# Splitting the first load, turning the taps earlier and re-ordering an SSM convolution and SwiGLU kernel on Trainium2

## The chip, the cores and the metric

The kernel runs on one core of one Trainium2 chip. The time is device time in microseconds (us), the median of three runs. A core has four compute engines that work side by side: TensorE (PE in the profile; its weight loads are listed as PEld), VectorE (DVE), ScalarE (ACT) and GpSimd (POOL). SyncE (SP) issues most transfers; a transfer issued by ACT stands in ACT's queue. The order of the instructions on each engine is written out by the program; the engines meet through semaphores.

## The reference

Sequences of 2048 rows with 512 channels go through two rounds of a convolution block A and a gated feed-forward block B, with the same weights in both rounds:

```python
def _A_ref(q, k, v, shift_k, ssm_k, ssm_D):
    k_shift = sum of k_pad[:, t:t + S, :] * shift_k[:, 3 - t] over the 4 taps
    kv = k_shift * v
    y = irfft(rfft(kv padded to 2S) * rfft(ssm_k padded to 2S))[:S] + kv * ssm_D
    return q * y

def _B_ref(x, w_gate, w_up, w_down):
    return (silu(x @ w_gate) * (x @ w_up)) @ w_down

x = A_q
x = x + _A_ref(layernorm(x), A_k, A_v, A_shift_k, A_ssm_k, A_ssm_D)
x = x + _B_ref(layernorm(x), B_w_gate, B_w_up, B_w_down)
x = x + _A_ref(layernorm(x), A_k, A_v, A_shift_k, A_ssm_k, A_ssm_D)
x = x + _B_ref(layernorm(x), B_w_gate, B_w_up, B_w_down)
```

(The first line of A and the FFT lines are condensed.) The tensors are bf16; w_gate and w_up are 512 x 1792, w_down is 1792 x 512. The convolution's result y is the same in both rounds, so it is computed once.

## The kernel before

**Tiling.** The 2048 rows are four blocks of 512 (NB = 4). In a block, partition p holds the rows 4p to 4p+3 (R = 4), so a block is a tile of 128 partitions x 4 rows x 512 channels. A unit of the feed-forward is (layer, block, half), two of the four rows of a block: 16 units of 256 rows.

**Convolution.** The long convolution is done in blocks. Each block of the filter h (ssm_k) and of kv gets a small Fourier spectrum by matmuls with cosine and sine tables (`fwd`, whose transposes `inv` serve the way back). Products of spectra are formed and added up on DVE, and matmuls with `inv` give y. h comes with channels on the partitions, and PE transposes it to `hs` (L511; copies out of PSUM at L521 to L527). The skip term D is added to row 0 of h there (`drow`, L524). k is transposed in the same way (L400, copies L406/L408) to `kT`, which has a pad of zeros in front (L394).

**The four taps.** `shift_mul` (L531) computes the shifted sum of k on PE: per row and per group of 128 channels (dt = 0 to 3), four matmuls of kT with a diagonal matrix `dg` that carries one tap of 128 channels. The taps are loaded as rows (`tapR`, L1087), turned on PE (L1153), copied to `tapT` and `tapF` on DVE (L1155, L1156), and 16 diagonals are made from the identity (L1166 to L1173), dt by dt on the engine that the string DGE names: D for DVE, A for ACT, P for POOL. The product with v (L558) gives kv.

**Feed-forward.** The normalised x is transposed to zT. For each pair of 128 columns of the 1792, PE computes gate and up (L997, recorded at the helper line L345), ACT applies SiLU (L1000) and copies up to ht (L1004), DVE multiplies (L1007), and PE adds up the down projection in PSUM (L1020). Elsewhere ACT copies the result to dn (L1056) and DVE adds it to x (L1059). In the last unit, (1, 3, 1), the residual x is put into PSUM first by matmuls with the identity (L979); the second of its two rows is split into two halves of 256 channels, one in `pds[1]`, one in `pds[2]`, and its last copies (L1027, L1033) write x straight from PSUM, with the output transfers at L1029 and L1036.

**Order.** The code first lists all operations (`plan.add`), each with its engine, an estimated cost, an estimated latency for transfers (`lat`), and what it reads and writes. ORDER gives each operation its position in one sequence; `Plan.order` sorts by it and places the operations in time by the estimates, `Plan.issue` (L251) writes them out in that sequence. So ORDER fixes each engine's queue, and the buffers of each ring follow from it. LH0 and LK0 are the estimated latencies of the first h and the first k.

**Fillers.** In `issue`, where PE's planned start lies more than 0.5 us behind its last end and before 32 us, matmuls on constants (`wm`, L1288) are written in, one per 0.106 us of planned gap. They go to the first PSUM slot, in the order pf, pd, pc, that is free at that time.

**The start of the queues.** ACT issues the loads of the taps and of drow. SP issues h of block 0 (L376, 512 KB in one transfer, since H_SPLIT is False), k, v, x of block 0, h and v of block 1, the gate weights, the two transposes of the tables (L1177), then k of block 1 and the other weights. POOL makes constants and the identity, then three diagonals, the pad of kT and a fourth diagonal.

Of the kernel before, what the change touches and what calls it, by code (L numbers as in the profile page):

```python
# [29 lines left out]
LH0 = 3.6  # L30
LK0 = 4.3
# [8 lines left out]
DGE = 'DDAP'  # L40
SHE = "DDDD"
PAIRS = ((0,), (2,), (1,), (3,))
H_SPLIT = False
# [8 lines left out]
    4, 74, 3, 1, 2, 22, 16, 12, 14, 0, 13, 15, 40, 7, 6, 5, 8, 9, 17, 11, 18, 19, 10, 20, 21, 25, 41, 42, 56, 57, 34, 35, 33, 36, 31, 32, 29, 30, 51,  # L52
    53, 52, 70, 38, 39, 45, 48, 23, 24, 26, 64, 60, 46, 44, 61, 55, 43, 66, 76, 73, 47, 37, 82, 27, 28, 62, 63, 58, 68, 54, 65, 49, 50, 59, 69, 79,
    168, 199, 216, 243, 275, 75, 93, 94, 95, 96, 80, 89, 90, 91, 92, 77, 78, 81, 84, 85, 97, 98, 99, 100, 101, 104, 103, 105, 110, 125, 134, 147, 148,
    149, 166, 178, 71, 102, 111, 116, 117, 119, 120, 121, 67, 87, 83, 88, 72, 86, 106, 107, 108, 109, 112, 113, 114, 130, 131, 132, 144, 145, 146,
    139, 140, 141, 135, 136, 137, 126, 127, 128, 118, 122, 124, 123, 115, 133, 152, 155, 161, 156, 170, 175, 138, 129, 153, 154, 142, 143, 150, 151,
    158, 160, 157, 163, 159, 164, 171, 179, 162, 165, 197, 198, 188, 211, 212, 213, 176, 167, 177, 182, 219, 227, 169, 173, 172, 174, 180, 181, 183,
    184, 189, 190, 228, 229, 208, 209, 191, 231, 210, 185, 195, 186, 192, 193, 187, 196, 194, 202, 203, 220, 224, 225, 226, 221, 222, 238, 223, 230,
    232, 242, 233, 246, 247, 268, 263, 269, 267, 270, 271, 273, 274, 272, 281, 283, 284, 304, 316, 317, 311, 312, 248, 255, 257, 256, 259, 258, 261,
    260, 214, 215, 234, 205, 206, 207, 200, 201, 204, 217, 218, 236, 325, 326, 235, 249, 321, 324, 295, 296, 308, 309, 290, 292, 299, 300, 237, 285,  # L60
    327, 329, 354, 355, 368, 367, 276, 302, 375, 613, 303, 262, 305, 319, 320, 353, 369, 373, 374, 418, 432, 413, 433, 434, 460, 459, 465, 502, 473,
    495, 494, 514, 522, 524, 556, 557, 523, 542, 536, 500, 581, 650, 626, 651, 264, 265, 244, 245, 239, 240, 250, 251, 266, 323, 322, 252, 253, 241,
    254, 278, 288, 286, 287, 289, 336, 331, 291, 294, 293, 306, 297, 298, 279, 280, 307, 337, 332, 301, 310, 313, 314, 315, 338, 333, 339, 334, 342,
    352, 366, 350, 351, 360, 361, 346, 357, 378, 422, 399, 386, 387, 402, 403, 385, 388, 364, 365, 407, 423, 430, 406, 411, 404, 405, 384, 395, 396,
    397, 412, 424, 431, 340, 341, 344, 345, 371, 437, 439, 438, 440, 441, 347, 343, 348, 356, 349, 358, 359, 370, 376, 377, 381, 382, 383, 389, 391,
    390, 393, 394, 409, 410, 419, 420, 414, 415, 451, 452, 444, 445, 453, 461, 463, 462, 464, 466, 467, 471, 470, 472, 476, 477, 501, 545, 496, 544,
    447, 450, 448, 449, 488, 489, 487, 492, 493, 509, 506, 468, 469, 491, 498, 479, 481, 456, 457, 499, 510, 534, 482, 511, 454, 486, 504, 512, 474,
    475, 517, 537, 535, 518, 519, 505, 515, 541, 584, 563, 585, 596, 624, 667, 625, 427, 421, 428, 458, 478, 484, 485, 528, 530, 532, 533, 551, 553,
    538, 540, 554, 564, 573, 574, 565, 567, 400, 503, 277, 282, 531, 560, 599, 561, 619, 620, 622, 623, 621, 648, 649, 661, 662, 723, 689, 724, 318,
    330, 335, 328, 362, 380, 392, 379, 363, 398, 372, 401, 436, 480, 483, 490, 416, 417, 408, 426, 442, 443, 425, 429, 521, 548, 598, 597, 552, 601,  # L70
    603, 618, 529, 507, 513, 516, 497, 446, 435, 520, 569, 526, 571, 508, 455, 525, 527, 539, 555, 572, 578, 617, 612, 580, 579, 652, 641, 727, 728,
    717, 718, 683, 688, 676, 677, 665, 684, 643, 644, 642, 656, 731, 732, 733, 734, 778, 765, 769, 781, 674, 543, 750, 1069, 668, 657, 670, 671, 697,
    678, 698, 699, 796, 790, 805, 806, 807, 834, 835, 846, 880, 847, 891, 895, 888, 881, 892, 894, 889, 890, 896, 910, 902, 905, 925, 900, 926, 938,
    943, 949, 996, 995, 999, 1000, 1023, 1006, 1024, 1067, 582, 583, 591, 592, 568, 586, 558, 559, 600, 610, 629, 590, 595, 549, 550, 588, 589, 593,
# [31 lines left out]
    1498, 1495, 1496, 1500, 1501, 1470, 1493, 1502, 1508, 1507, 1503, 1504, 1479, 1480, 1494, 1499, 1491, 1492, 1509, 1510, 1511, 1481, 1482, 1460,  # L106
    1461, 1483, 1522, 1520, 1532, 1538, 1539, 1561, 1540, 1551, 1555, 1535, 1536, 1513, 1519, 1533, 1534, 1514, 1523, 1537, 1552, 1556, 1521, 1530,
    1515, 1516, 1528, 1529, 1524, 1525, 1531, 1553, 1557, 1543, 1544, 1526, 1527, 1541, 1542, 1548, 1549, 1550, 1554, 1562, 1545, 1546, 1517, 1518,
    1547, 1558, 1563, 1566, 1559, 1560, 1564, 1565, 1567, 1568,
]  # L110
R = 4

# [1209 lines left out]
```

## Time and profile before

| | us |
|---|---|
| median of 3 runs (344.92 to 345.08) | 344.96 |
| the profiled execution: its own time | 345.11 |
| its span (first to last record) | 343.3 |
| PE busy | 338.7 |
| DVE busy | 282.3 |
| ACT busy | 253.2 |
| POOL busy | 39.7 |
| first transposes of h on PE | 4.83 |
| first FFN matmul on PE | 33.45 |
| last matmul issued, end of PE's work | 340.3 |

The profile describes one execution. A timeline row gives the start and the length in us, the engine, the line of the code, the operation, "output<-inputs", shapes and how many were merged; in brackets, how long the engine sat idle before it and what released it. "SPq" and "ACTq" are DMA issues. A row of the chain of waits has only start, length, engine, tile and line. The end of a matmul is modelled, so a row of n matmuls lasts longer than n times their rate by the depth of the pipe; the starts are measured.

### The profile page before, as it was taken

The page shows a single profiled execution, that of the slowest core. Times are in us where ns is not written, and L with a number is a line of the kernel's source. Part 1 is how long each engine was busy: PE and PEld are TensorE (multiplying, and loading weights), DVE is VectorE, ACT ScalarE, POOL GpSimd, SP SyncE. Part 2 cuts the span into 40 slices and gives each one's busy share as a digit, 9 for nine tenths or more (in the row PEclk, how much of TensorE's full clock was granted, in tenths as well). Part 3 has the DMA queues.
Part 4 walks back from the last instruction along what each step waited for, and adds up shares of the span by engine and source line. Part 5 has one row for each costly group of instructions (what it writes and reads, how often), then busy time and mean ns, then how long its engine had stood idle before and what let it go on. Part 6 is the DMA issues. An engine that isn't in the chain of part 4 may idle for free.

```text
span 343.3 us, 6617 instructions
## 1 busy us (share of the span) xinstructions
PE 338.7 (99%) x2624; PEld 248.5 (72%) x2624; DVE 282.3 (82%) x481; ACT 253.2 (74%) x505; POOL 39.7 (12%) x46
## 2 busy tenths in 40 slices
PE   8999999999999999999999999999999999999996
PEld 7747867768686767768587768768675877777684
DVE  7999999999999999999999999989987523637030
ACT  6899999999984868867999955959464654546271
POOL 4000110103010101221010100100601000000000
PEclk9999999999999999999999999999999999999999
DMA  7999016130117156010101057000101010100001
GB/s 289 326 317 320 3 28 98 31 94 0 34 31 124 36 119 124 7 26 2 32 18 32 15 153 93 15 18 0 33 0 43 18 52 2 31 15 17 15 17 47
DMA packets 42089, 22.96 MB, mean 67 GB/s; under 512 B 33861, under 2 KB 39882, under 8 KB 42058
## 3 DMA queue, kind: packets, MB, share of 16 engines
q1 hardware_dynamic: 41904, 22.47, 26.3%
q8 instruction: 20, 0.33, 0.4%
q14 instruction: 11, 0.09, 0.1%
q10 hardware_dynamic: 154, 0.07, 0.1%
HBM read 12.33 MB, written 2.10 MB: 42 GB/s over the span
## 4 chain that ended last, share of the span: by engine, by line
PE 66%; DVE 29%; ACT 2%; issue 1%; DMA 1%; DVEq 0%
PE pf L345 38%; PE pd L1020 18%; PE ps L345 6%; DVE ht L1007 4%; DVE bnst L843 3%; DVE t L687 3%; DVE t L691 3%; DVE t L699 2%; DVE m L574 2%; DVE Z L701 2%; PE ps L492 2%; DMA zT<-z 1%; PE ps L831 1%; PE wm L1288 1%; DVE ka L642 1%
## 5 line engine op out<-in xcount | busy, mean ns | idle before, releaser
L345 PE MATMUL pf<-zT,wg_sb 128*128 128x256 bf16 x896 | 110.1, 273 | 0.1
L345 PE MATMUL pf<-zT,wu_sb 128*128 128x256 bf16 x896 | 109.6, 273 | 0.1
L1020 PE MATMUL pd<-wd_sb,ht 128*128 128x512 bf16 (+1 forms) x462 | 104.2, 373 | 0.0
L345 PEld LDWEIGHTS <-wg_sb 128*128 128x128 bf16 x896 | 87.6, 98 | 16.6 <-issue 0.6
L345 PEld LDWEIGHTS <-wu_sb 128*128 128x128 bf16 x896 | 87.6, 98 | 16.2 <-DMA zT<-z 0.5
L1004 ACT CAST ht<-pf 128x512 bf16<-128x512 f32 x112 | 64.5, 591 | 22.1 <-PE pf L345 21.8
L1000 ACT ACTIVATE sg<-pf 128x512 bf16<-128x512 f32 x112 | 65.8, 605 | 17.2 <-PE pf L345 13.4
L1020 PEld LDWEIGHTS <-ht 128*128 128x128 bf16 x462 | 45.1, 98 | 44.2 <-DVE ht L1007 0.6
L1007 DVE TENSOR_TENSOR ht<-ht,sg 128x1024 bf16<-128x1024 bf16 (+1 forms) x64 | 39.1, 618 | 22.5 <-ACT sg L1000 18.7
L848 POOL TENSOR_TENSOR rstd<-ve,nhalf 128x2 f32<-128x2 f32 x24 | 27.7, 1155 | 211.0 <-DVE ve L846 201.5
L1056 ACT CAST dn<-pd 128x512 bf16<-128x512 f32 x30 | 17.3, 591 | 31.9 <-PE pd L1020 21.8
L843 DVE BATCH_NORM_STATS2 bnst<-xc 128x6 f32<-128x512 bf16 x48 | 31.6, 685 | 0.7
L687 DVE TENSOR_TENSOR t<-X,G 128x2048 bf16<-128x2048 bf16 x18 | 22.0, 1220 | 0.1
L691 DVE TENSOR_TENSOR t<-X,G 128x2048 bf16<-128x2048 bf16 x18 | 21.9, 1217 | 0.0
L1059 DVE TENSOR_TENSOR xc<-xc,dn 128x1024 bf16<-128x1024 bf16 x15 | 10.2, 681 | 11.6 <-ACT dn L1056 11.6
L453 ACT ACTIVATE X<-ps 128x512 bf16<-128x512 f32 x32 | 19.2, 608 | 0.7 <-PE ps L492 0.5
L874 POOL TENSOR_TENSOR rstd<-ve,nhalf 128x2 f32<-128x2 f32 x8 | 8.6, 1075 | 60.5 <-ACT ve L872 60.5
L920 DVE TENSOR_TENSOR n<-n,Yk 128x1024 bf16<-128x1024 bf16 x15 | 10.3, 690 | 6.4 <-ACT Yk L725 5.4
L701 DVE TENSOR_TENSOR Z<-Z,t 128x2048 bf16<-128x2048 bf16 x12 | 14.7, 1224 | 0.3
L699 DVE TENSOR_TENSOR t<-t,t 128x2048 bf16<-128x2048 bf16 x12 | 14.7, 1223 | 0.3
L453 ACT ACTIVATE H<-ps 128x512 bf16<-128x512 f32 x24 | 13.9, 618 | 0.0
L345 PE MATMUL ps<-hs,fwd 128*128 128x512 bf16 x40 | 12.8, 379 | 0.5 <-ACT hs L521 0.3
(105 smaller groups left out, 323.7 us busy)
## 6 DMA issues: line engine op xcount, KB each, us to landing
hn<-in_A_ssm_k_dram SPq DMA_DIRECT2D x4, 512.0 KB, 5.3
vt<-in_A_v_dram SPq DMA_DIRECT2D x4, 512.0 KB, 5.2
xc<-in_A_q_dram SPq DMA_DIRECT2D x4, 512.0 KB, 6.0
out_dram<-xc SPq DMA_DIRECT2D x15, 128.0 KB, 1.8
wg_sb<-in_B_w_gate_dram SPq DMA_DIRECT2D x1, 1792.0 KB
wu_sb<-in_B_w_up_dram SPq DMA_DIRECT2D x1, 1792.0 KB, 7.6
wd_sb<-in_B_w_down_dram SPq DMA_DIRECT2D x1, 1280.0 KB, 12.7
kn<-in_A_k_dram SPq DMA_DIRECT2D x1, 512.0 KB, 4.4
```

Source lines behind the costliest of these rows:

```text
L345: nc.tensor.matmul(o, lhsT=lhsT, rhs=rhs, start=(n == 0), stop=(n == len(terms) - 1))
L453: add("ACT", act(D), lambda: nc.scalar.activation(out=view(), in_=ps.t[:], func=ACT.Copy, scale=scale), r=[ps], w=[(buf, keys)], conv=conv)
L687: dve(n * D, lambda t1=t1, part=part: nc.vector.tensor_mul(out=t1.t[:], in0=x.t[:, sl, 0, :], in1=g.t[:, sl, part, :]), [(x, key(slots, (0 ...
L691: dve(n * D, lambda t2=t2, part=part: nc.vector.tensor_mul(out=t2.t[:], in0=x.t[:, sl, 1, :], in1=g.t[:, sl, 1 - part, :]), [(x, key(slots ...
L699: dve(n * D, lambda t1=t1, t2=t2, comb=comb: nc.vector.tensor_tensor(out=t1.t[:], in0=t1.t[:], in1=t2.t[:], op=comb), [t2], [t1], conv=conv)
L701: dve(n * D, lambda t1=t1, part=part: nc.vector.tensor_add(out=z.t[:, sl, part, :], in0=z.t[:, sl, part, :], in1=t1.t[:]), [t1], [zk], con ...
L843: add("DVE", 0.6, lambda st=st, i=i: nc.vector.bn_stats(out=st.t[:], in_=xs[c].t[:, i, :]), r=[(xs[c], (i,))], w=[st])
L848: add("POOL", pw, lambda: nc.gpsimd.tensor_tensor(out=rstd.t[:], in0=ve.t[:], in1=nhalf.t[:].to_broadcast((P, n)), op=ALU.pow), r=[ve, nha ...
L1000: add("ACT", act(D), lambda ps=ps, o=o, sg=sg: nc.scalar.activation(out=sg.t[:, o:o + 2, :], in_=ps.t[:], func=ACT.Silu), r=[ps], w=[(sg, ...
L1004: add("ACT", act(D), lambda ps=ps, o=o, ht=ht: nc.scalar.copy(out=ht.t[:, o:o + 2, :], in_=ps.t[:]), r=[ps], w=[(ht, (o // 2,))], due=(uni ...
L1007: dve(n * W, lambda sg=sg, ht=ht: nc.vector.tensor_mul(out=ht.t[:], in0=ht.t[:], in1=sg.t[:]), [sg], [ht], due=(unit, k / pairs, 0.0, "h"))
L1020: nc.tensor.matmul((pds[o] if not cs.start else pds[HP]).t[:, cs], lhsT=ht.t[:, q, o * P:(o + 1) * P], rhs=wt["d"].t[:, ft, cs], start=(ft ...
```

## The change

- **First h in two transfers** (H_SPLIT = True): channels 0 to 255, then 256 to 511, 256 KB each, issued one behind the other by SP. PE transposes each row of h in two operations, one per half. The estimated latencies of h and k change with it.
- **Taps turned at once:** the estimated latency of their load goes from 2.6 to 1.1, so that the plan sees them earlier.
- **Diagonals:** DGE goes from 'DDAP' to 'DPAP'; the four of dt = 1 move from DVE to POOL, which makes eight.
- **Fillers** go to the free PSUM slot whose next use lies furthest ahead.
- **Last unit:** only the second half of the second row gets its residual by an identity matmul. The first row and the first half of the second are added by DVE when their sums are done; ACT copies the last half.
- **ORDER** is a new table for all operations (1573 instead of 1569).

```diff
-LH0 = 3.6
-LK0 = 4.3
+LH0 = 3.35
+LK0 = 4.0
...
-DGE = 'DDAP'
+DGE = 'DPAP'
...
-H_SPLIT = False
+H_SPLIT = True
...
 ORDER = [
-    4, 74, 3, 1, 2, 22, 16, 12, 14, 0, 13, 15, 40, 7, 6, 5, 8, 9, 17, 11, 18, 19, 10, 20, 21, 25, 41, 42, 56, 57, 34, 35, 33, 36, 31, 32, 29, 30, 51,
+    1, 127, 7, 0, 3, 9, 17, 2, 8, 4, 5, 6, 50, 51, 11, 13, 10, 12, 14, 18, 19, 16, 15, 22, 27, 28, 38, 43, 52, 53, 59, 30, 44, 55, 33, 46, 47, 29, 40,
...
     def issue(self, seq, place, when, warm_until, warm):
         t, busy = 0.0, {}
+        slots = [(r, i) for r in ("pf", "pd", "pc") for i in range(self.rings[r])]
...
             if o.eng == "PE":
-                if start < warm_until and start - t > 0.5:
-                    for ring, i in [(r, i) for r in ("pf", "pd", "pc") for i in range(self.rings[r])]:
-                        if busy.get((ring, i), 0.0) <= t:
-                            n = int((start - max(t, 0.3)) / 0.106)
-                            if n > 0:
-                                warm(ring, i, n)
-                            break
+                n = int((start - max(t, 0.3)) / 0.106)
+                free = [s for s in slots if busy.get(s, 0.0) <= t]
+                if start < warm_until and start - t > 0.5 and n > 0 and free:
+                    nxt = {s: 1e9 for s in free}
+                    for b, i in place.items():
+                        a = min(when[q][0] for q in b.ops)
+                        if (b.ring, i) in nxt and a >= t:
+                            nxt[b.ring, i] = min(nxt[b.ring, i], a)
+                    warm(*max(free, key=nxt.get), n)
...
         if b == 0 and H_SPLIT:
+            o = None
             for n in range(2):
                 sl = slice(2 * n, 2 * n + 2)
                 o = add(eng, 0.5, lambda sl=sl: q.dma_start(out=hn[b].t[:, sl], in_=h3[:, sl, 0:L]), w=[(hn[b], (n,))],
-                        lat=LH0 - 0.75 if n == 0 else LH0 - 0.45, due=due, after=after)
+                        lat=LH0 - 1.0 if n == 0 else LH0 - 0.45, due=due, after=list(after) + [o] * n)
...
-        if xpe:
+        if unit == LAST_UNIT:
+            cs, i = slice(D // 2, D), row(h, HP - 1)
+            add("PE", pe(1, D // 2), lambda: nc.tensor.matmul(pds[HP].t[:, cs], lhsT=ident.t[:], rhs=x.t[:, i, cs], start=True, stop=False),
+                r=[(x, (i,)), ident], w=[pds[HP]], due=(unit, 2 / pairs, 1.9, None))
+        elif xpe:
...
-                                                 start=(ft == 0 and not xpe), stop=(ft == NF - 1))
+                                                 start=(ft == 0 and not (cs.start if unit == LAST_UNIT else xpe)), stop=(ft == NF - 1))
...
-            add("ACT", act(D), lambda: nc.scalar.copy(out=x.t[:, row(h, 0), :], in_=pds[0].t[:]), r=[pds[0]], w=[(x, (row(h, 0),))],
-                due=(unit, 1.0, 3.0, "h"))
+            add("DVE", tt1(D), lambda: nc.vector.tensor_add(out=x.t[:, row(h, 0), :], in0=x.t[:, row(h, 0), :], in1=pds[0].t[:]), r=[pds[0]],
+                w=[(x, (row(h, 0),))], due=(unit, 1.0, 3.0, "h"))
...
-                copy = nc.scalar.copy if eng == "ACT" else nc.vector.tensor_copy
-                add(eng, 0.35, lambda cs=cs, copy=copy, half_=half_: copy(out=x.t[:, i, cs], in_=pds[HP if half_ else o].t[:, cs]), r=[pds[HP if half_ else o]],
+                def finish(cs=cs, half_=half_):
+                    if half_:
+                        nc.scalar.copy(out=x.t[:, i, cs], in_=pds[HP].t[:, cs])
+                    else:
+                        nc.vector.tensor_add(out=x.t[:, i, cs], in0=x.t[:, i, cs], in1=pds[o].t[:, cs])
+                add(eng, 0.35, finish, r=[pds[HP if half_ else o], (x, (i,))],
...
         tr = add("ACT", 0.42, lambda: nc.scalar.dma_start(out=tapR.t[:], in_=A_shift_k.rearrange("(dt p) j -> dt p j", p=P)), w=[tapR],
-                 lat=2.6, due=-71)
+                 lat=1.1, due=-71)
```

## The prediction

> **What bounds the kernel now.** I read the page's busy times first, then the chain of waits of the first 36 us, the stage table, the timeline of the start and the timeline of the last 12 us.
>
> ```profile
> PE 338.7 (99%) x2624; PEld 248.5 (72%) x2624; DVE 282.3 (82%) x481; ACT 253.2 (74%) x505; POOL 39.7 (12%) x46
> ```
>
> PE is busy for 99% of the span, but its ends are modelled, so I check it by rate. In the chain, eight 256-column matmuls take 0.87 us and four of 512 columns 0.86 us, so 0.109 and 0.2157 us each.
>
> ```profile
> 43.64 0.87 PE pf L345 x8
> 63.21 0.86 PE pd L1020 x4
> 221.75 5.13 PE L1020 MATMUL pd<-wd_sb,ht 128*128 128x512 bf16 x23
> 226.93 1.05 PE L345 MATMUL pf<-zT,wu_sb 128*128 128x256 bf16 x8
> 243.27 1.89 PE L1020 MATMUL pd<-wd_sb,ht 128*128 128x512 bf16 x8
> 245.27 1.47 PE L345 MATMUL pf<-zT,wg_sb 128*128 128x256 bf16 x12
> ```
>
> The last four lines are timeline rows. 221.75 + 23 x 0.2157 = 226.71, and PE goes on at 226.93: 0.22 us lost to the DMA of zT. 243.27 + 8 x 0.2157 = 245.00, next 245.27: 0.27 us lost. From the first FFN matmul (33.45) to the end (340.3) I find no other loss over 0.1 us. So after 33.45 an edit counts only if it takes PE work away, or makes or fills a wait of PE; the DVE work saved there is free.
>
> ```profile
> 13.86:26.59 12.73, 12.34 (x75) 6.11 (x74) 12.54 (x25) 11.74 (x24) 0.72 (x1) 1.00 1.11 292
> 26.59:33.45 6.86, 6.85 (x86) 5.13 (x85) 6.43 (x17) 6.86 (x16) 0.81 (x1) 1.00 1.03 348
> ```
>
> ```profile
> 13.86 0.69 DVE L558 TENSOR_TENSOR vt<-ps,vt 128x512 bf16<-128x512 f32 x1 [0.20 <-PE ps L345]
> ```
>
> Two stages (their length, then busy PE, PEld, DVE, ACT, POOL) and a timeline row. From the last product kv (L558, 13.86) to the first FFN matmul DVE is busy 12.54 of 12.73 and 6.43 of 6.86 us, with only work that leads to the first z (spectra, products, sums, statistics). So the FFN starts 19.6 us after that DVE product, whatever PE does meanwhile; and the product waits for PE's shift matmuls, which stand behind the transposes of h. PE itself loses about 1.5 us to waits and 0.55 us to ten fillers between 22.4 and 31.5.
>
> ```profile
> 0.76 2.83 PE L1288 MATMUL wm<-const-bfloat16-1.0 128*128 128x128 bf16 x25 [0.76 <-PEq L1306]
> 3.52 0.29 PE L1153 MATMUL pt<-ident,tapR 4*128 4x4 bf16 x4
> 3.74 1.03 PE L1288 MATMUL wm<-const-bfloat16-1.0 128*128 128x128 bf16 x8
> 4.83 1.18 PE L511 MATMUL pt<-ident,hn 128*128 128x128 bf16 x16
> 5.38 1.07 ACT L521 COPY hs<-pt 128x512 bf16<-128x512 bf16 x2 [0.87 <-PE pt L511]
> ```
>
> h was issued at 0.72 and landed 3.6 us later, at 4.3; PE turned it from 4.83. The fillers (wm) go at about 0.106 us each, half the speed of the transposes of k later (12 in 0.83 us).
>
> **The end: -0.32 us.** Three identity matmuls (L979: one of 512 columns, two of 256) become one of 256. 0.2157 + 0.109 = 0.32 us of PE's stream goes. Does it show at the end?
>
> ```profile
> 333.60 0.38 PE L979 MATMUL pd<-xc,ident 128*128 128x512 bf16 x1
> 333.81 2.75 PE L1020 MATMUL pd<-wd_sb,ht 128*128 128x512 bf16 x12
> 334.42 0.69 DVE L1007 TENSOR_TENSOR ht<-ht,sg 128x1024 bf16<-128x1024 bf16 x1 [0.44 <-ACT ht L1004]
> 340.09 0.42 DVE L1033 CAST xc<-pd 128x256 bf16<-128x256 f32 x1 [4.99 <-PE pd L1020]
> 340.31 0.37 ACT L1033 CAST xc<-pd 128x256 bf16<-128x256 f32 x1 [0.72 <-PE pd L1020]
> ```
>
> The last h tile is ready at 335.11. PE has ten other matmuls for that row in front of it (333.81 + 10 x 0.2157 = 335.97), 0.86 us of cover, more than the 0.32 taken. Behind the last matmul the ACT copy of the second half (0.37) and its transfer stay. The first half becomes a DVE add out of PSUM: the trace has none of 256 columns, but at 512 columns an operation with a PSUM and an SBUF operand (L558, 0.69) costs what a one-operand copy does (L408, 0.69), so I take the 0.42 of the present cast; twice that would end at 340.09 - 0.32 + 0.84 = 340.6, about where ACT's half ends. The row-0 add (0.69 for ACT's 0.59) starts near 338.7 and is done before DVE is wanted at 339.8. With the cover gone this part would be worth nothing: 0 to -0.32.
>
> **The start: -0.1 us (-0.6 to +0.4).**
> - h in two transfers. The bytes are the same; SP issues one DMA more (0.46 + 0.06 us), so k, v, x, the second blocks and wg are issued 0.5 us later. k landed 4.4 us after its issue at 1.24, 1.3 us after h, as long as its 512 KB need behind h; v and x follow likewise. Their data, not their issue, set these landings: 0. Behind wg SP issues the two transposes of the tables (4.53 to 15.99), which then begin some 0.25 us later. The second lands 13.1 us after its issue at 10.3, at 23.4; the first inverse matmul is at 24.11. Cover 0.7, then 0.45; without it, 0.25 us on PE.
> - Fillers. Their number follows the gaps of the written plan, at one per 0.106 us (a count that the code fixes, no time of the chip). The planned arrival of the taps moves from 0.42 + 2.6 to 0.42 + 1.1, so 14 of the 25 before the turn go; some 10 stand between it and the first half of h (planned 0.5 + 2.35 = 2.85), and 6 before the second half (planned 1.1 + 2.9 = 4.0). The taps' packets had all moved by 2.0 us, so the turn comes near 2.1 instead of 3.52. Then: 10 fillers to 3.4; eight transposes of the first half at the slow 0.107, to 4.3; 6 fillers to 4.9; the second half, r3 and r1 first, from 4.9 instead of 4.83. The first copy to hs (5.38 now) comes at about 5.4, though the last transposes end some 0.5 us earlier. What the early half gains, slow transposes and fillers eat. Without them r3 would be ready 0.3 and r2 0.75 us sooner: -0.6 is my bound for a start that follows the landings.
> - The new filler slot (the free one whose next use is furthest off). Now h's first transpose waits for the fillers to drain out of its own slot: last filler at 3.74 + 7 x 0.103 = 4.46, transpose at 4.83, 0.26 us more than one filler. That wait goes: -0.2, within the -0.6.
> - Diagonals. tapF comes after three of the second four phase operations, near 3.1 + 0.17; POOL starts at about 3.45 instead of 4.45. By the new order it makes six diagonals, the pad of kT, two more: 3.45 + 8 x 0.61 + 0.15 = 8.5. The first shift matmul, which reads the pad (7.3), is at 9.65 now, and those of the third and fourth POOL diagonals' blocks come a microsecond later. Cover 1 to 3 us: 0. DVE gets rid of 4 x 0.25 us before the shift matmuls, where PE, not DVE, is the chain (PE has seven pairs of h, 16 transposes of k and 64 shift matmuls without a gap from 6.17 to 13.6): 0.
>
> What speaks against more work on POOL:
>
> ```profile
> 3.94 0.25 DVE L1131 TENSOR_SCALAR fwd<-fwd 128x384 bf16<-128x384 bf16 x1
> 6.39 0.41 DVE L1131 TENSOR_SCALAR fwd<-fwd 128x384 bf16<-128x384 bf16 x1
> 6.32 0.62 POOL L1171 TENSOR_SCALAR dg<-ident,tapF 128x128 bf16<-128x128 bf16 x1
> 240.99 4.21 POOL L848 TENSOR_TENSOR rstd<-ve,nhalf 128x2 f32<-128x2 f32 x1 [1.58 <-DVE ve L846]
> ```
>
> The same DVE operation takes 0.25 us alone and 0.41 beside a POOL diagonal, and a two-element POOL operation took 4.21 us while DVE was full (0.72 at 19.47). I charge one such 0.16 us to the copies of hs. [...]
>
> Together: -0.2 for the slot, -0.1 for earlier last transposes, +0.16 for the sharing, rounded to -0.1.
>
> **The new order: -0.1 us (-0.5 to +0.8).** It can't take work from PE. It can remove the 0.22 and 0.27 us waits and some of the 2 us before 33.45, but there DVE and ACT are full too (ACT 11.74 of 12.73 and 6.86 of 6.86 us), so little can be moved forward. It can as well place new waits for zT or ht; the two we see are the size of one, and three such are +0.8. I take a fifth of the gain.
>
> **Sum** against the profiled execution (345.11; span 343.3 and 1.8 around it): 345.11 - 0.32 - 0.1 - 0.1 = 344.6; the median shown is 0.15 lower, so **344.5**, with 344.0 to 345.0 as its own range.
>
> **Rivals.**
> 1. The start follows the landings and the order fills the waits: -0.32 - 0.6 - 0.4 = -1.3, 343.65. For it: fillers are passed at half the time once PE is at its full rate, and DVE and ACT are busy only 7.70 and 7.54 us of the 9.03 before 13.86. Against: the fillers' counts above.
> 2. POOL's diagonals come late (slower). If DVE's constants and copies hold POOL as they held rstd (mean 1.155 for 0.72 us, 1.6 times), a diagonal takes 0.98 and the last is there at 3.45 + 7.8 + 0.25 = 11.5, just when its shift matmul is due; from there each 0.1 us per diagonal is 0.8 us. At 1.2 us each: 13.3, PE 1.8 us late, kv and the FFN with it: 344.96 - 0.32 + 1.8 = 346.4. Against: the four now took 0.60 to 0.62, one of them beside DVE work.
> 3. The order brings new waits of PE after 33.45: five of 0.25 us, 344.96 - 0.4 + 1.25 = 345.8. Against: PE has fillers of its own there, conv matmuls; for: only two such waits now, few to lose and many to gain.
>
> **Chances.** Forecast 0.45, rival 1 0.31, rival 2 0.10, rival 3 0.14. A change under 0.2% (0.69 us: 344.27 to 345.65) can't be told from none here. Of the forecast's 0.45 about 0.08 lies below 344.27; of rival 1 and 3 some 0.04 lies inside. So faster 0.37, same 0.41, slower 0.22. The range 343.5 to 345.9 leaves out rival 2, half of rival 3's upper tail and a little of rival 1: under 0.2.
>
> **What would show it.** In the changed trace: the last matmul 0.32 us earlier against the first of the last unit; taps turned near 2.1; the first hs copy at 5.4 (rival 1: 5.0); kv of the last row at 13.8; POOL's last diagonal at 8.5 with 0.6 each (rival 2: 0.9 or more, and PE waiting before L345 with dg); first FFN matmul at 33.4; PE waits over 0.1 us after it summing to 0.4 (rival 3: over 1). The forecast is wrong if kv's last row moves by more than 0.4 us, or if the waits after 33.4 change by more than 0.5.

## The result and the profile after

| | us |
|---|---|
| after: median of 22 runs (344.06 to 346.99) | 345.42 |
| before, on the same chips: median of 22 runs (344.17 to 345.99) | 344.70 |
| ratio after / before | 1.0022, 95% interval 1.0013 to 1.0032 |
| forecast | 344.5 (343.5 to 345.9) |

The kernel became slower by about 0.2%. It also scatters more: the standard deviation of its runs is 0.8 us, that of before 0.4. Together with three later sets on other chips (58 runs of after, 121 of before) the medians are 345.17 and 344.73, the deviations 0.93 and 0.35.

The profiled execution of after was one of its quick ones: 344.37 us, span 342.6. Its page and the timeline of its start on PE:

```profile
PE 337.9 (99%) x2622; PEld 247.9 (72%) x2622; DVE 281.7 (82%) x478; ACT 252.7 (74%) x504; POOL 39.3 (11%) x50
```

```profile
0.76 1.33 PE L1298 MATMUL wm<-const-bfloat16-1.0 128*128 128x128 bf16 x11 [0.76 <-PEq L1316]
2.18 0.29 PE L1163 MATMUL pt<-ident,tapR 4*128 4x4 bf16 x4
2.40 1.25 PE L1298 MATMUL wm<-const-bfloat16-1.0 128*128 128x128 bf16 x10
3.50 0.93 PE L515 MATMUL pt<-ident,hn 128*128 128x128 bf16 x8
4.27 0.51 PE L1298 MATMUL wm<-const-bfloat16-1.0 128*128 128x128 bf16 x6
5.17 0.64 PE L515 MATMUL pt<-ident,hn 128*128 128x128 bf16 x8 [0.39 <-DMA hn<-in_A_ssm_k_dram]
5.64 0.51 PE L1298 MATMUL wm<-const-bfloat16-1.0 128*128 128x128 bf16 x6
6.10 0.59 PE L348 MATMUL ps<-hs,fwd 128*128 128x512 bf16 x2
```

The taps are turned at 2.18 and the first half of h at 3.50, nearly as forecast (2.1, 3.4). The second half is waited for until 5.17. The first hs matmul starts at 6.10; before it was 6.17. The early half has gained 0.07 us. The chain of waits of the first 8 us (start, length, what) says why:

```profile
0.72 0.46 SPq L377
1.18 0.06 issue
1.24 3.88 DMA hn<-in_A_ssm_k_dram
5.12 0.05 issue
```

The second transfer was issued at 1.24 and took 3.88 us for 256 KB: it landed at 5.12. Before, all 512 KB were there at 4.37. In the three further executions of the table below the second half landed earlier, at 4.22, 4.58 and 4.36 us, before PE came to it; there PE's rate is what was late.

The same rows in three further executions of the same kernel:

| execution | taps turned | first half of h | last slow matmul | first hs matmul | first FFN matmul | its time |
|---|---|---|---|---|---|---|
| before | 3.52 | 4.83 | 4.9 | 6.17 | 33.45 | 345.11 |
| after | 2.18 | 3.50 | 4.0 | 6.10 | 33.16 | 344.37 |
| after_again | 2.17 | 3.55 | 6.95 | 6.52 | 33.95 | 345.46 |
| after_third | 3.01 | 4.28 | 7.05 | 7.26 | 34.32 | 345.51 |
| after_fourth | 3.00 | 4.26 | 6.2 | 6.91 | 33.96 | 345.27 |

"Slow" is a matmul of 128 columns of 0.29 us or more, 0.107 us after its neighbour (at full rate 0.22 and 0.056), or one of 512 columns of 0.48 or more (0.38). Timeline of PE in after_third:

```profile
0.76 1.33 PE L1298 MATMUL wm<-const-bfloat16-1.0 128*128 128x128 bf16 x11 [0.76 <-PEq L1316]
3.01 0.29 PE L1163 MATMUL pt<-ident,tapR 4*128 4x4 bf16 x4 [0.92 <-DMA tapR<-in_A_shift_k_dram]
3.24 1.25 PE L1298 MATMUL wm<-const-bfloat16-1.0 128*128 128x128 bf16 x10
4.28 1.06 PE L515 MATMUL pt<-ident,hn 128*128 128x128 bf16 x8
5.13 0.85 PE L1298 MATMUL wm<-const-bfloat16-1.0 128*128 128x128 bf16 x6
5.77 1.06 PE L515 MATMUL pt<-ident,hn 128*128 128x128 bf16 x8
6.62 0.80 PE L1298 MATMUL wm<-const-bfloat16-1.0 128*128 128x128 bf16 x6
```

Two things differ from the quick execution. The taps landed near 3.0, and PE, which has nothing it may do before them, stood idle for 0.92 us. And six fillers take 0.85 us instead of 0.51, eight transposes 1.06 instead of 0.64: PE was at half its rate until 7.1. From the first hs matmul to the FFN it is 27.06 us in three of them and 27.43 in after_again, whose first hs matmuls were slow; the time less the start of the FFN is 311.2 to 311.5 in all four. So what differs between these four lies before about 7 us. No run of after above 345.6 us has a trace.

The diagonals (timeline of GpSimd) and the end (timelines of PE, DVE and ACT) of the quick execution:

```profile
3.44 3.98 POOL L1181 TENSOR_SCALAR dg<-ident,tapF 128x128 bf16<-128x128 bf16 x6 [1.78 <-DVE tapF L1166]
7.37 0.15 POOL L398 MEMSET kTb<- 128x64 bf16 x1
7.49 1.18 POOL L1181 TENSOR_SCALAR dg<-ident,tapF 128x128 bf16<-128x128 bf16 x2
```

```profile
333.25 6.24 PE L1026 MATMUL pd<-wd_sb,ht 128*128 128x256 bf16 x42
338.22 0.69 DVE L1033 TENSOR_TENSOR xc<-xc,pd 128x512 bf16<-128x512 bf16 x1 [2.14 <-PE pd L1026]
339.31 0.42 DVE L1042 TENSOR_TENSOR xc<-xc,pd 128x256 bf16<-128x256 bf16 x1 [0.40 <-PE pd L1026]
339.53 0.37 ACT L1040 CAST xc<-pd 128x256 bf16<-128x256 f32 x1 [4.51 <-PE pd L1026]
```

GpSimd's first two diagonals took 0.87 and 0.79 us, the other six 0.60 to 0.63; it is done at 8.67, and the first shift matmul starts at 10.01. At the end the DVE adds take 0.69 and 0.42 us, the price forecast, and ACT's last copy still ends last.

The page's stages up to the FFN (length, then busy PE, PEld, DVE, ACT, POOL):

```profile
13.80:26.33 12.53, 12.18 (x74) 6.14 (x73) 12.50 (x26) 11.63 (x25) 1.20 (x1) 1.00 1.11 287
26.33:33.16 6.83, 6.83 (x86) 5.19 (x85) 6.41 (x17) 6.81 (x15) 0.81 (x1) 1.00 1.08 389
```

DVE is as full as before. From the first spectrum of kv (L496, 14.01) to the FFN it is 19.14 us, before 19.35.

### The profile page after: what moved, and what is told of

It is laid out like the page before. It is cut to its first block, busy times and chain, and to the rows that moved or that the text cites. A ratio compares the mean times of both kernels' runs of the same rounds, so it can differ in the third digit from the quotient of the medians.

```text
span 342.6 us, 6598 instructions
## 1 busy us (share of the span) xinstructions
PE 337.9 (99%) x2622; PEld 247.9 (72%) x2622; DVE 281.7 (82%) x478; ACT 252.7 (74%) x504; POOL 39.3 (11%) x50
## 4 chain that ended last, share of the span: by engine, by line
PE 97%; DMA 1%; ACT 1%; SPq 0%; issue 0%
PE pf L348 57%; PE pd L1026 28%; PE ps L348 7%; PE ps L496 2%; DMA hn<-in_A_ssm_k_dram 1%; PE ps L835 1%; ACT H L457 0%; PE pt L515 0%; ACT hs L525 0%; PE pt L404 0%; ACT X L457 0%; PE ptz L958 0%; SPq L377 0%; ACT xc L1040 0%; PE wm L1298 0%
## 5 line engine op out<-in xcount | busy, mean ns | idle before, releaser
L1006 ACT ACTIVATE sg<-pf 128x512 bf16<-128x512 f32 x112 | 66.8, 609 | 22.8 <-PE pf L348 18.3
L852 POOL TENSOR_TENSOR rstd<-ve,nhalf 128x2 f32<-128x2 f32 x24 | 25.7, 1073 | 223.1 <-DVE ve L850 223.1
L878 POOL TENSOR_TENSOR rstd<-ve,nhalf 128x2 f32<-128x2 f32 x8 | 7.5, 940 | 48.8 <-ACT ve L876 48.8
```

The source lines that it names most:

```text
L852: add("POOL", pw, lambda: nc.gpsimd.tensor_tensor(out=rstd.t[:], in0=ve.t[:], in1=nhalf.t[:].to_broadcast((P, n)), op=ALU.pow), r=[ve, nha ...
L1006: add("ACT", act(D), lambda ps=ps, o=o, sg=sg: nc.scalar.activation(out=sg.t[:, o:o + 2, :], in_=ps.t[:], func=ACT.Silu), r=[ps], w=[(sg, ...
```

## The experiments

Times are medians, each against the kernel before on the same chip. The diffs are condensed to the part that matters. Three theories were stated at first. A: PE's rate in the first microseconds, set by the fillers, makes the scatter and the loss. B: h (its landings) sets the start. C: the new order makes waits later on.

**The changed kernel again**, three times, on three chips, unchanged.

> The changed kernel once more, for a second execution's trace. Its 22 times spread from 344.06 to 346.99 us, those of before from 344.17 to 345.99, and the trace shown is of one of its fastest (344.37). Theory A (PE's rate): the moment at which PE's matmuls go from 0.107 to 0.056 us per 128 columns moves from execution to execution (4.15 us in the trace shown), and a slower execution has it later, 1 to 3 us later for 1 to 2 us of time. Theory B (h): the moment is the same, but the second half of h lands later than 5.12 us. Theory C (order): the start is the same, and waits of PE after 33 us sum to 1 us more than the 0.3 us of the trace shown.

> The changed kernel once more, beside the three below on one chip. So far its FFN starts at 33.16 us in a 344.37 us execution, with PE at its full rate from 4.15 us, and at 33.95 in a 345.46 us execution, with the full rate from 7.0. Theory A: time minus FFN start is again 311.2 to 311.5, whatever the time, and the FFN start follows the moment of the full rate. Theory C: FFN start unchanged, the rest longer.

> The changed kernel once more, to stand beside the other three on one chip. Its medians so far were 345.42, 344.61 and 345.15 us (before 344.70, 344.87, 344.70): expected 344.6 to 345.5 with a standard deviation of 0.5 to 0.9, so that the others are compared with it here and not with another set.

Measured: 344.61 (before 344.87; deviation 0.92), 345.15 (344.70; 0.56) and 345.58 (344.76; 1.17). The ratios are 1.0003 (0.9987 to 1.0019), 1.0011 (1.0000 to 1.0021) and 1.0037 (1.0017 to 1.0057). Time less FFN start in after_third is 345.51 - 34.32 = 311.19. A's account of after_third is right only in part: there PE's rate was late behind a late landing of the taps, which A had not named.

**h in one transfer again, all else the change's.**

```diff
-q.dma_start(out=hn[b].t[:, sl], in_=h3[:, sl, 0:L])
+q.dma_start(out=hn[b].t[:], in_=h3[:, :, 0:L]) if n == 0 else None
```

> The changed kernel with the first h in one transfer again (the same order, the second issue left out). Theory B: h lands at about 4.4 instead of 3.5 and 5.1, the last transposes of h end some 0.6 us earlier, and the median falls by about 0.5 us with a narrower spread. Theories A and C: within 0.2 us of the changed kernel, with the same spread.

Measured 346.53 (before 344.87), 1.9 above after_again: the wrong way for B. Timeline of PE:

```profile
4.34 1.04 PE L515 MATMUL pt<-ident,hn 128*128 128x128 bf16 x8 [0.70 <-DMA hn<-in_A_ssm_k_dram]
5.17 0.85 PE L1298 MATMUL wm<-const-bfloat16-1.0 128*128 128x128 bf16 x6
5.81 1.06 PE L515 MATMUL pt<-ident,hn 128*128 128x128 bf16 x8
6.67 0.85 PE L1298 MATMUL wm<-const-bfloat16-1.0 128*128 128x128 bf16 x6
7.31 1.06 PE L348 MATMUL ps<-hs,fwd 128*128 128x512 bf16 x2
```

h is there at 4.3, but the fillers, counted for two halves, still stand between and behind the transposes, PE stood still for the landing, and it was slow until 9.0, the latest of all executions. So the landing alone doesn't set the start, and this run doesn't price the split.

**The taps behind 25 fillers again, h still in halves.**

```diff
-warm(*max(free, key=nxt.get), n)
+warm(*max(free, key=nxt.get), n + 14 if t == 0.0 else n)
```

> The changed kernel with 14 more fillers in front of the turn of the taps (25, as before), nothing else. Theory A: PE has no break before the h transposes, the rate rises as in before, the spread narrows to the 1.0 us of most runs of before and the median falls by 0.5 us or more, although the turn comes 1.4 us later. Theories B and C: not faster; the turn at 3.5, the first half of h transposed from about 4.7, tapF and GpSimd's diagonals 1.4 us later, hidden: 0 to +0.3 us.

Measured 345.10 (ratio 1.0015, 1.0005 to 1.0025), 0.49 above after_again's median, where A expected 0.5 or more below it. The early half's gain was gone (first half of h at 4.78). The deviation was 0.51 instead of 0.92, but after_third, unchanged, has 0.56, so that the late turn narrows the scatter isn't shown.

**The last unit alone, in the kernel before.**

```diff
-rhs=x.t[:, i, cs], start=True, stop=False) for cs in halves],
+rhs=x.t[:, i, cs], start=True, stop=False) for cs in halves
+if unit != LAST_UNIT or cs.start],
...
-nc.scalar.copy(out=x.t[:, row(h, 0), :], in_=pds[0].t[:])
+nc.vector.tensor_add(out=x.t[:, row(h, 0), :], in0=x.t[:, row(h, 0), :], in1=pds[0].t[:])
```

> The kernel before with the last unit of the changed one alone (two of the three identity matmuls gone, VectorE adds x). The forecast's term: -0.32 us against before, in all theories. If the cover at the end is gone or the add out of PSUM is dearer than the copy: 0 to -0.1.

Measured 344.59 against 344.87: -0.28 us. The ratio is 0.9994 (0.9985 to 1.0002), so the times alone don't settle it; the traces do. In the timeline of the last 12 us the eight matmuls of pf begin at 332.28 and ACT's last copy at 339.54, 7.26 us on; before it was 332.73 to 340.31, 7.58 us. The difference is 0.32.

```profile
335.74 0.27 PE L979 MATMUL pd<-xc,ident 128*128 128x256 bf16 x1
335.85 3.65 PE L1021 MATMUL pd<-wd_sb,ht 128*128 128x256 bf16 x30
339.54 0.37 ACT L1035 CAST xc<-pd 128x256 bf16<-128x256 f32 x1 [5.60 <-PE pd L1021]
```

**More and fewer fillers.** filled: 14 and 11 fillers in the first two stretches of after instead of 11 and 10. thinned: none in the second. before_thinned: 15 ahead of the taps of before instead of 25.

```diff
-warm(*max(free, key=nxt.get), n)
+n = max(0, n + (more.pop(0) if more else 0))
+if n: warm(*max(free, key=nxt.get), n)
```

more is [3, 1] in filled and [0, -10] in thinned. The moment that the expectation of filled speaks of is the one at which PE goes from 0.107 to 0.056 us per 128 columns.

> The changed kernel with 3 more fillers before the turn of the taps and 1 more before the first half of h, which end when PE has to wait anyhow: the breaks of 0.34 and 0.11 us go. [...] If the moment is chance alone (breaks this small don't matter): the spread stays near 3 us, the median within 0.2 of the changed kernel's on this chip.

> The changed kernel without the 10 fillers between the taps' turn and h's first half, so PE sits idle for 1.2 us there. Theory A: the full rate comes 2 to 3.4 us later than in the changed kernel, the median rises by 1 to 2 us. If only the landings count: no change, since PE waits for h with or without fillers.

> The kernel before with 15 instead of 25 fillers in front of the taps' turn, so PE sits idle from 2.5 to 3.5 us; order, transfers and all else as before. Theory A: the same loss without anything of the change, +1 to +2 us against before, and a spread of 2 us or more. If the cause of the spread is in the new order or in h's two transfers: no change from before.

Measured beside a before of 344.70 and an after of 345.15: filled 344.72, thinned 345.49, before_thinned 345.39 (1.0026, 1.0013 to 1.0039). Ten fillers less cost the kernel before 0.69 us though its h was turned 0.5 us earlier, at 4.33. Timeline of PE:

```profile
4.33 1.90 PE L511 MATMUL pt<-ident,hn 128*128 128x128 bf16 x16 [0.62 <-DMA hn<-in_A_ssm_k_dram]
6.02 1.87 PE L345 MATMUL ps<-hs,fwd 128*128 128x512 bf16 x4
```

In the trace of before the 16 transposes take 1.18 us and four hs matmuls 1.02: there the last slow matmul stands at 4.9, soon after h comes, in before_thinned at 7.3 (one execution each), and the ten fillers pay. In the changed kernel the effect is small: thinned is 0.34 above after_third, where A expected 1 to 2 us. Filling the gaps moved the median by 0.43, but the means are 0.07 apart, the ratios 1.0006 (0.9995 to 1.0017) and 1.0011 (1.0000 to 1.0021) overlap, and the deviation stayed at 0.63. So the fillers' worth is shown for before, and for after not.

**The taps behind the first half of h, in one unbroken stream.**

```diff
+for i, at in ((51, 33.1), (53, 33.2), (68, 33.3), (61, 33.4), (60, 33.5), (64, 33.6), (54, 33.7)):
+    ORDER[i] = at
...
+t, busy, k, more = 0.0, {}, 0, {0: 25, 5: 5, 9: 5}
...
```

(more gives the number of fillers at a place of PE's queue. turn_later_one_h has 34, 0 and 5, and h in one transfer.)

> After with the taps' turn (and the copy of the taps and the first diagonals) behind the four transposes of the first half of h, and the fillers dealt 25, 5 and 5 so that TensorE never stops before the hs matmuls. If the spread of after comes from the taps' landing at the head of TensorE's queue (turned at 2.2 us in two executions, at 3.0 in a third) and from the moment of TensorE's full rate, both are gone: fillers until about 3.4, first transposes of h 3.5, the second half when it lands at 5.1, full rate from 4.2 to 5.0, first FFN matmul 33.1 to 33.3, median 344.2 to 344.5 with a standard deviation of about 0.3 (after 0.5 to 0.9). If the spread is from elsewhere, median 344.6 to 345.4 and a deviation over 0.5, as after.

> The same with h in one transfer: fillers 34 ahead of the transposes of h, none between, 5 behind. If the split costs by its late second half (5.1 us where the whole lands at 4.3), all 8 transposes run from 4.3, end at 4.9, and hs is 0.1 to 0.3 us earlier: median 0.1 to 0.3 below turn_later. If the split is worth what it was made for, this is 0.1 to 0.4 us slower than turn_later. If only the fillers' stretch mattered, both are within 0.1.

Measured 345.48 and 346.24 (before 344.79): both expectations missed. The timeline of ACT in turn_later shows a wait of the experiment's own:

```profile
5.29 0.40 ACT L1181 ACTIVATE dg<-ident,tapF 128x128 bf16<-128x128 bf16 x1 [0.78 <-DVE tapF L1170]
5.60 0.56 ACT L529 COPY hs<-pt 128x512 bf16<-128x512 bf16 x1
6.06 0.40 ACT L1181 ACTIVATE dg<-ident,tapF 128x128 bf16<-128x128 bf16 x1
6.37 0.57 ACT L529 COPY hs<-pt 128x512 bf16<-128x512 bf16 x1
```

The late taps put the diagonals of ACT (and of DVE) in front of the copies to hs, and PE waited 0.74 us for these (first hs matmul at 6.90), though it was at full rate from 4.5. These two say nothing of the split; they show that whoever turns the taps late must put the diagonals behind hs.

**The dealing of the diagonals undone in after.**

```diff
-DGE = 'DPAP'
+DGE = 'DDAP'
```

> After with the diagonals dealt as before (two of three by VectorE). If GpSimd's diagonals are hidden, as the trace of after has it (last one at 8.67 us, first shift matmul 10.0), 0.0 +- 0.2 us against after_again and after_third together (344.6 and 345.1), with their spread of 0.5 to 0.9. [...]

Measured 346.86 (before 344.79), 1.7 to 2.3 above after_again and after_third. In the new order the four diagonals of dt = 1 stand so late in DVE's queue that the last is made at 12.59, and PE waits for it:

```profile
12.89 1.28 PE L348 MATMUL ps<-dg,kTb 128*128 128x128 bf16 x20 [0.52 <-DVE dg L1181]
```

From the first hs matmul to the first spectrum of kv it takes 9.48 us instead of 7.92, 1.56 more: that wait and 15 fillers that the plan puts in front of it. So the new order can't do without GpSimd's diagonals; that doesn't say that they are free.

**Two parts alone that should gain: the last unit and the filler slot, in the kernel before.** (The edit does what these two parts of the change do.)

> Before with two of the change's parts alone: the last unit's residual and the filler slot rule (which takes away the 0.26 us wait of the h transposes behind the fillers' slot). If the parts stand as measured (end -0.28 to -0.3, slot -0.1 to -0.3), first FFN matmul 33.0 to 33.3, median 344.2 to 344.4, so 0.4 to 0.6 below before. If the slot's wait only moves behind the next wait, 344.5, as the last unit's part alone (344.59).

Measured 344.31 against 344.79, ratio 0.9986 (0.9977 to 0.9995), deviation 0.34. It is the only variant whose interval lies wholly below before. Its traced execution doesn't show the slot at work, since h landed only at 4.82 there. The trace of last_slot_dpap (below; the same rule, h there at 4.32) does:

```profile
3.74 1.04 PE L1296 MATMUL wm<-const-bfloat16-1.0 128*128 128x128 bf16 x8
4.57 1.28 PE L514 MATMUL pt<-ident,hn 128*128 128x128 bf16 x16
```

The transposes of h start at 4.57, one filler's time behind the last filler, instead of at 4.83.

**Both start edits undone in after, and each of them alone in before.**

In after, besides the one transfer of h shown above:

```diff
-t, busy = 0.0, {}
+t, busy, k, more = 0.0, {}, 0, {0: 25, 1: 8, 5: 0, 9: 0}
```

In before, for the early taps:

```diff
-t, busy = 0.0, {}
+t, busy, few = 0.0, {}, [11, 22]
...
-n = int((start - max(t, 0.3)) / 0.106)
+n = few.pop(0) if few else int((start - max(t, 0.3)) / 0.106)
```

In before, for the split:

```diff
-q.dma_start(out=hn[b].t[:], in_=h3[:, :, b * L:(b + 1) * L])
+[q.dma_start(out=hn[b].t[:, sl], in_=h3[:, sl, b * L:(b + 1) * L])
+ for sl in ((slice(0, 2), slice(2, 4)) if b == 0 else (slice(0, 4),))]
```

> The changed kernel with the start of before: h in one transfer, 25 fillers, then the taps, 8 fillers, the eight transposes of h at 4.83 without fillers between them or behind them. All else is the change's: order, diagonals on GpSimd, last unit. If the start is what costs, hs matmuls begin at 6.1 as in before, the FFN at 6.1 + 27.06 = 33.1 to 33.3, and the median is 344.1 to 344.4, 0.4 to 0.6 below before with its small deviation of 0.3. If a later part costs (order, or the diagonals), it stays within 0.2 of after_fourth.

> The kernel before with one thing changed: the taps turned behind 11 fillers instead of 25, then 22 fillers instead of 8. If the taps' turn at the head of TensorE's queue costs (their landing exposed, at 2.1 us in most and 3.0 in some executions, and the fillers broken by 0.3 to 1.2 us, so that the full rate comes later), median 0.2 to 0.8 above before and deviation 0.5 or more (before 0.3). If the taps' place is harmless and the split is the cost, 0.0 +- 0.15.

> The kernel before with one thing changed: the first load of h as two transfers, the later loads issued 0.5 us later, taps and fillers as they were. If the second half lands at 5.1 as in after, the first four transposes (eight matmuls) run from 4.83 to about 5.3 and nothing waits or 0.1: median 0.0 to +0.15 against before. If the split is the cost by itself (the halves and the loads behind them late), +0.3 to +0.8.

Measured, beside before at 344.76 and after_fourth at 345.58: late_taps_one_h 345.05 (ratio 1.0008, 0.9997 to 1.0020; deviation 0.52), before_early_taps 345.26 (ratio 1.0029, 1.0016 to 1.0042; deviation 0.65), before_split 345.24 (1.0014, 1.0004 to 1.0024; 0.41). Each start edit alone costs about 0.5 us, and taking both away gives 0.53 back (on deviations of 1.17 and 0.52, and not the sum of the two). Of the 0.50 of before_early_taps some 0.2 are my fillers: 22 behind the taps ran to 4.8, and h was turned at 5.06 instead of 4.83. The split's 0.47 came against an expectation of 0.0 to 0.15. Its profiled execution was a quick one (344.74), with both halves there by 4.54 and PE fast from 3.8, so it doesn't show the split at its worst (timeline of PE, then of PE's weight loads):

```profile
4.46 1.10 PE L512 MATMUL pt<-ident,hn 128*128 128x128 bf16 x16
5.72 1.02 PE L345 MATMUL ps<-hs,fwd 128*128 128x512 bf16 x4 [0.16 <-DVE hs L528]
6.77 0.40 PE L401 MATMUL pt<-ident,kn 128*128 128x128 bf16 x4
```

```profile
6.77 0.23 PEld L401 LDWEIGHTS <-kn 128*128 128x128 bf16 x4 [0.52 <-DMA kn<-in_A_k_dram]
```

Even here PE loses 0.2 us to k: it landed at 6.73, its transposes begin at 6.77 instead of 6.58, and from the first hs matmul to the first spectrum of kv it is 8.12 us instead of 7.92. In the ten traces with the split k landed at 6.43 to 8.19 us (median 7.5), in the ten without it at 5.39 to 6.30 (median 5.7). Before has k's first transposes at 7.04, so a k at 7.5 would cost its order some 0.45 us, as much as was measured. That is an estimate from these rows: no slower execution of before_split was traced. In after the new order has k's transposes 0.06 us behind the landing (8.25 and 8.19), in the other three executions 1.8 us or more behind it.

late_taps_one_h should have been at 344.1 to 344.4. It has the end's 0.3 us and is still 0.3 above before, so about 0.6 us were left to find. Its traced execution (345.63) was slow on PE until 6.2, and it has a wait behind the FFN's start that the traces of after don't have (timeline of PE):

```profile
225.19 1.04 PE L1028 MATMUL pd<-wd_sb,ht 128*128 128x512 bf16 x4 [0.39 <-DVE ht L1015]
```

It is the third rival's kind of wait. PE goes on 0.55 us later than its rate allows, and from the first FFN matmul to the last matmul it takes 306.74 us, where after took 306.06 to 306.33. turn_later has the same wait (0.55), late_taps one of 0.38 at 73.4.

**The diagonals alone, in before and in before_last_slot.** (DGE = 'DPAP', nothing else.)

> The kernel before with the dealing of the diagonals alone changed (DPAP). If they are hidden: six on GpSimd from 4.45 to 8.1 us, the pad of kT at 8.2, the last near 9.5, first shift matmul at 9.65 and PE without a gap from hs to the first spectrum of kv (7.92 us, as before and as after): 0.0 +- 0.15 against before. [...]

> before_last_slot (344.31 beside a before of 344.79) with DPAP. If the diagonals are hidden, 0.4 to 0.5 below before again, within 0.15 of before_last_slot's distance; if VectorE's freed microsecond brings the FFN forward, 0.6 to 0.8 below; if they cost, 0.0 to 0.3 below.

Measured, beside before at 344.44: before_dpap 345.57 (ratio 1.0023, 1.0013 to 1.0033), last_slot_dpap 344.88 (1.0009, 0.9999 to 1.0018). The first is +1.13 by medians, +0.79 by means; the second stands 0.44 above its before where before_last_slot stood 0.48 below, so +0.92. The diagonals cost, in both pairs. But not where I looked: in before_dpap GpSimd's last is done at 9.4, PE goes from hs (6.45) to the first spectrum of kv (14.37) in 7.92 us as in before, and the FFN follows 19.35 us later, as in before. (That hs is 0.28 us later than in before is PE's rate, slow to 6.1 in this execution.) The one later wait that the two traces have and the other kernels in the old order hardly have is this one, in before_dpap and in last_slot_dpap:

```profile
245.76 0.93 PE L345 MATMUL pf<-zT,wg_sb 128*128 128x256 bf16 x7 [0.55 <-DMA zT<-z]
```

```profile
245.26 1.47 PE L348 MATMUL pf<-zT,wg_sb 128*128 128x256 bf16 x12 [0.49 <-DMA zT<-z]
```

In these two the DMAs of zT landed 3.4 to 3.5 us after their issue; in the five other kernels of the old order at that place it was 2.4 to 3.2, with 0.27 us of waiting in before and none in the rest. The instructions of PE, ACT and SP are the same in before and before_dpap, in the same order, so nothing in the program ties this wait to the diagonals. And after, with the same dealing, lands them in 2.5 to 3.0. Against the same kernel without the new dealing, PE loses 0.4 us more there in before_dpap and 0.65 more in last_slot_dpap (by the starts of its matmuls), so in these executions the wait is a part of the price. The price of the diagonals is measured in the old order only, and its cause is open.

## Why the prediction was wrong

It said -0.46 against 344.96 and the change is some +0.4 to +0.8 (+0.72 in its own set, +0.44 over all sets). The time lies inside the stated range; the direction was wrong. The sum failed in the start and in the diagonals; the end and the slot held.

- **The end, -0.32: right.** -0.28 measured alone (within the noise of the times), 0.32 in the trace, DVE adds at 0.42 and 0.69 us as priced.
- **The start, -0.1 (-0.6 to +0.4): the failing step.** It measured about +0.5 (after_fourth less late_taps_one_h; +0.8 by means), and each of its two edits alone about +0.5 in the kernel before. Three of its sentences fell. "The taps' packets had all moved by 2.0 us, so the turn comes near 2.1 instead of 3.52": this was read from one execution of before, in which the turn stood at 3.52 behind 25 fillers and hid the landing. At the head of PE's queue the landing is exposed, and it was 3.0 in two executions of four. "Their data, not their issue, set these landings: 0": k was issued 0.5 us later and landed 1 to 2 us later (median 7.5 instead of 5.7). "10 fillers to 3.4; eight transposes of the first half at the slow 0.107, to 4.3; 6 fillers to 4.9; the second half, r3 and r1 first, from 4.9 instead of 4.83": I took the count of the plan and let PE become fast at 4.9 as before, but in three of four executions it was slow to 6.2 or 7, though the second half was there by 4.6 in these three. Every matmul between the first half and hs, twelve fillers among them, is on the path and takes 0.107 us instead of 0.056 as long as PE is slow. The whole range was worked out from one execution's landings and one moment of full rate; the change makes the path depend on both.
- **The filler slot, -0.2: right in mechanism.** In last_slot_dpap the transposes of h start 0.26 us earlier, at 4.57. The time, 0.48 - 0.28 = 0.20, is a difference of two sets on two chips and within their noise.
- **The diagonals, 0: wrong in the time, right in the trace's place.** The last was done at 8.67 (forecast 8.5), no matmul waits for one, and the copies of hs took 0.42 us as before, so not even the 0.16 charged for sharing came: DVE's operation on fwd, 0.41 us beside a diagonal of GpSimd before, took 0.24 and 0.26 beside them in after, and no run shows that the two engines share anything. It was GpSimd's own work that took longer: 0.87 and 0.79 us for its first two diagonals, beside DVE's work from 3.49 to 4.68, where the forecast had 0.61 for all. And the row with 4.21 us "while DVE was full (0.72 at 19.47)" was misread: at 19.47 DVE was as full (L676 from 18.92 to 20.81). Alone in the old order they cost 0.8 to 1.1 us all the same; the one wait seen with them there, for zT at 245, isn't in after, so that this price holds for after as well is argued, not shown.
- **The new order, -0.1:** about 0 by the four traces of after. It gains 0.2 us between the first spectrum of kv and the FFN in all four executions (19.14 or 19.15 for 19.35). From FFN to last matmul after takes 306.06 to 306.33, and the old order with the new end (before_last, before_last_slot) 305.89 and 305.73: what the order wins ahead of the FFN it gives back.
- **The rivals.** The first (start follows the landings, 343.65) is what the quickest run of after_again, 343.92, comes near. The second named the right part, GpSimd, with the wrong mechanism: two of its diagonals were slow, but none was late. The third (waits after the FFN) isn't seen in the quick execution (0.11 and 0.17 us), but it comes in some: 0.30 us before zT in after_again, one wait of 0.38 to 0.55 us in late_taps, late_taps_one_h and turn_later, which have the same order.

Added up: -0.28 for the end, -0.20 for the slot, +0.53 for the start. The change is +0.72, so some +0.7 are left for the diagonals and the order together, which is also what late_taps_one_h shows (0.29 above before with the end's and the slot's gain in it: +0.77). The 0.8 to 1.1 us of the diagonals alone would fill it, and so, in part, would the waits of the new order; no run tells the two apart. The parts come from several chips, and with deviations of 1.17 and 0.52 in twelve runs each the start alone is known to no better than some 0.7 us. Open are how the diagonals act, whether they do so in the new order, where ddap shows that it can't do without them, how often the new order's waits come, and whether the late k is all that the split costs.

## What to carry to other kernels

Work that waits for a transfer and is moved to the head of an engine's queue buys the transfer's whole scatter (here the taps were turned at 2.17 to 3.01 us): ask how late that transfer can land, not when it landed once. While PE is at half rate, fillers ahead of the first real work can be worth more than an earlier start (ten fillers less cost before 0.69 us), and fillers behind it cost twice as much each (0.107 us instead of 0.056). Splitting one load moves the loads behind it too (k landed at a median of 7.5 us instead of 5.7): look at who needs those. Try each part of a bundle by itself: here two of the parts made the kernel before 0.5 us faster, and the others hid them.

## What the runs showed of the hardware that was not expected

- **The moment of PE's full rate.** The last slow matmul stood between 3.3 and 9.0 us in twenty executions whose first filler is always at 0.76. Where PE stood still for less than 0.5 us before it (by the starts of its matmuls), it came at 3.3 to 6.95 (14 executions, median 4.9); where it stood still for 0.85 or more, at 6.2 to 9.0 (6 executions, median 7.05). A late moment also leaves more time to stand still in, so the halves aren't fully independent; before and before_thinned (4.9 and 7.3) fit, with one execution each. The clock column of the windows reads 1.00 all the while, but only because it counts time without a clock record as full. The first record of the granted clock in the trace itself comes 0.1 to 0.6 us behind the last slow matmul in all nineteen traces that have one: at 5.13 us in before, at 4.18, 7.23, 7.24 and 6.41 in the four executions of after, at 9.21 in one_h. In the first group (thirteen of the fourteen) it lies between 3.83 and 7.23, over all nineteen between 3.83 and 9.21. On its two sides PE takes 0.107 and 0.056 us per 128 columns; what sets the moment, and why it differs between executions of one kernel, no run shows.
- **What the split did to the landings.** The whole h (512 KB, issued at 0.72) landed at 4.11 to 4.82 us in ten traces. As two transfers of 256 KB (issued at 0.72 and 1.24) its first half landed at 3.44 to 3.96 and its second at 4.22 to 5.23 in ten others, so the second half is later than the whole in some executions only. The next load, k, landed 1 to 2 us later: 6.43 to 8.19 instead of 5.39 to 6.30. A load of 4 KB (the taps), issued at 0.72, let PE turn it at 2.17 and 2.18 in two executions of after and at 3.00 and 3.01 in two.
